# Ten more weight tasks beside the first block's attention, and all but the first eight ordered behind the newest scaled row maxima

## The chip, the cores and the metric

The kernel runs on one core of a Trainium2 chip. The metric is the device time of one execution in microseconds (us). The engines named below are PE (matmuls), DVE (vector), ACT (activations), POOL (GpSimd) and SP, whose queue issues the DMA transfers.

## What is computed

Causal attention with a forget bias, over 4 batches, 8 heads, 576 positions and heads of 64, then two MLP blocks over the 2304 resulting rows of 512:

```python
scores = scale * q @ k.T + minimum(-(cum_i - cum_j), 0), causal; attn = softmax(scores); x = attn @ v
xn = x / rms(x) * rms_g                      # first MLP: d_ff 1536
x = (silu(xn @ w_gate) * (xn @ w_val)) @ w_out
h = x @ w_in                                 # second MLP: d_ff 2048
out = (h - tanh(h)) @ w_out2
```

## The kernel before

Every matmul operand that needs more than half precision is held as a high and a low float16 part, so that one product is three matmuls (lines 676 to 678).

**Attention** goes over 20 tiles T of up to 128 query rows (five in a batch, T0 to T4 the first batch's). For a tile the row maxima of the scores are found first: score matmuls into a "sm" bank (lines 384 to 399) and a reduction on DVE (lines 386, 394, 400). `emit_rt` scales them to a high and a low half (lines 410 and 411, both on DVE), transposes them on PE (414) and sends them by DMA into the query operand. Line 411's instruction is kept as `last_r[0]`: the newest scaled row maxima. Then come, in units of one to four heads, the transposed scores (435, 436), the exponentials (443, ACT), the mask (445, POOL) and the value matmuls (477 for the first batch, in float32). `emit_norm` normalizes a tile's rows in some ten short dependent steps and sends them through transposing DMAs (530, 531) into XT, the operand of the first MLP. `step()` runs the attention's generator by one unit.

**The first MLP** goes over six blocks of 384 rows; block 0 is the tiles T0 to T2. A block has 28 groups: twelve pairs of a gate half (`up1_g`) and a value half (`up1_v`), twelve matmuls each, and four down groups of 36. Each group takes one of two PSUM banks with the tag "mm", and gives it back when DVE or ACT has read it (lines 694, 703, 714).

**Weights.** The weights come as float64. `w1_tasks` is a list of 54 tasks in six column groups, gate and value of three column thirds in turn: g0, v0, g1, v1, g2, v2. A column group is four pieces, one chain and four splits. A piece is a transfer of 512 KB into a raw slot (line 540), three DVE instructions that make float32 of it (542 to 544), a square on ACT into the raw slot (573) and a matmul that sums the squares into an "mm" bank, which all four pieces share (589). There are six raw slots; piece n uses slot n mod 6. The chain reduces that bank on DVE (593) and makes the scale. A split writes the high part on ACT (558) and the low part on DVE (559). `wo_tasks` has 29 such tasks for the down weights. Pair f of a block needs g and v of column third f // 4.

**What sets the order.** The program is traced in the order in which the Python code runs; a scheduler with a simulated timeline then orders each engine's instructions at compile time, so that later work is pulled into gaps where its operands allow. Buffers are handed out by the tile pools. `tc.issue_after(ins)` gives each instruction traced in its block, on the engine of `ins`, a place behind `ins` on that engine; with `last_r[0]` that engine is DVE. The order on every engine is fixed when the kernel runs.

**The loop around the change.** Two weight tasks come first, then the maxima of T0, T1 and T2 and two attention steps. The `while` loop at line 936 then runs steps 3 to 16, until T2 is normalized. T3's maxima are traced within steps 7 to 12, so from step 12 on `last_r[0]` is T3's. One weight task follows each step: the loop takes fourteen of the sixteen in `left`, line 944 the other two, and g0 and v0 are complete. In block 0 of the first MLP, two weight tasks follow each group (line 959), and line 953 first brings up what the next column third needs; when the list is empty, six of the down weights' tasks follow each group.

Of the kernel before, what the change touches and what calls it, by code (L numbers as in the profile page):

```python
# [40 lines left out]
def tile_forget_attention_moe_moe2(ctx, tc, qa, qb, kt, va, vb, va0, vb0, s, wg, wv, wo, rg, win, wo2, out):  # L41
# [315 lines left out]
    last_r = [None]  # L357
# [371 lines left out]
    def run_tasks(lst, n):  # L729
        while n > 0 and lst:  # L730
            lst.pop(0)()
            n -= 1
# [124 lines left out]
    def v_first():  # L857
      with hold():
        vstate[0] = const.tile([128, H], FP32, name="vone")
        V.memset(vstate[0], 1.0)  # L860
        for hh in range(2):
            v32 = VT[hh].bitcast(FP32)
            SY.dma_start(out=v32[:, 0:16, :], in_=va0[hh])
            SY.dma_start(out=v32[0:64, 16:20, :], in_=vb0[hh])
# [22 lines left out]
        SY.dma_start(out=cpd, in_=CP)  # L887
    prep_q(0)
    v_first()
    left = [16]  # L890

    def rest_of_batch0():
        for hh in range(2):
            conv_kc(0, hh, k0, 384, S)
            conv_k2(0, hh, k0, 384, S)

    gen = attn_gen()
    steps = [0]
    total = sum(len(units(T)) for T in range(20)) + 2

    def step():
        try:
            next(gen)
            steps[0] += 1
        except StopIteration:
            pass

    def need(T):
        return sum(len(units(x)) for x in range(T + 1)) + 2
# [26 lines left out]
    while last0 not in done_norm:  # L936
        step()
        if steps[0] == 4:
            rest_of_batch0()
        n = min(left[0], 1)  # L940
        left[0] -= n
        with tc.issue_after(last_r[0]) if left[0] < 8 else ExitStack():
            run_tasks(wt, n)
    run_tasks(wt, left[0])
    wot = wo_tasks(raw_p)
    for j in range(NBLK - 1):
        last = BLOCK_TILES[j + 1][1] - 1
        s0 = steps[0]
        n = min(need(last), total) - s0
# [244 lines left out]
```

## Time and profile before

| | us |
|---|---|
| median of three runs | 1087.5 |
| lowest and highest of them | 1084.29, 1088.48 |
| the profiled execution | 1086.19 |
| its span, first to last instruction | 1084.4 |
| PE busy in the span | 993.0 |
| DVE busy | 621.8 |
| ACT busy | 604.1 |
| POOL busy | 281.9 |

The busy times are sums over stages with different limits, so they have to be read by stretch of the span. A granted TensorE clock of 1.00 is 2.4 GHz and one of 0.50 is 1.2 GHz; a value between is the mean of a stretch in which it changed. "Idle before" is the time in which an engine did nothing ahead of an instruction, and the arrow names what ended it.

### The profile page before, as it was taken

Reading aid. Unit: us, or ns where it says so; the run is one execution under the profiler, and the core shown is the slowest. Engines: PE = TensorE matmul, PEld = TensorE weight load, DVE = VectorE, ACT = ScalarE, POOL = GpSimd, SP = SyncE. Lnnn points to the kernel's source line nnn. Section 1 sums busy time; section 2 is a strip of 40 time slices with the busy share of each in tenths; the row PEclk is TensorE's granted clock in tenths of the full one; section 3 lists DMA queues with packets and bytes.
Section 4 is the critical chain, followed back from the end, with each engine's and each line's share of the span. In section 5 each row is a group of like instructions: output and inputs, shape, how many; then the busy total and the mean of one; then the engine's idle time right before and its main releaser. Section 6 shows DMA issues by size and latency. Waiting matters only on the chain.

```text
span 1084.4 us, 19355 instructions
## 1 busy us (share of the span) xinstructions
PE 993.0 (92%) x7576; PEld 631.0 (58%) x7576; DVE 621.8 (57%) x1421; ACT 604.1 (56%) x1176; POOL 281.9 (26%) x377
## 2 busy tenths in 40 slices
PE   1488878899889999899999899999999999999998
PEld 1377545465556666556566556666666666666665
DVE  8987998966573540674543878485341605234250
ACT  6587668785854662767566447365342515243240
POOL 5122356424652450745345102100000000000000
PEclk9976989899999999999999999999999999999999
DMA  8714333330101212110100960141010010100000
GB/s 268 271 36 110 143 108 113 97 118 21 40 22 50 59 21 82 32 26 22 47 19 11 329 205 1 52 163 45 15 37 24 1 51 8 44 15 8 23 1 30
DMA packets 47517, 75.04 MB, mean 69 GB/s; under 512 B 25506, under 2 KB 33282, under 8 KB 46914
## 3 DMA queue, kind: packets, MB, share of 16 engines
q1 hardware_dynamic: 47426, 73.81, 21.5%
q8 instruction: 59, 0.97, 0.4%
q14 instruction: 32, 0.26, 0.1%
HBM read 59.42 MB, written 9.55 MB: 64 GB/s over the span
## 4 chain that ended last, share of the span: by engine, by line
PE 70%; DVE 15%; ACT 4%; DMA 4%; issue 4%; POOL 3%; SPq 0%; ACTq 0%; DVEq 0%; POOLq 0%
PE m L676 13%; PE m L678 13%; PE m L677 13%; PE mm L676 7%; PE mm L678 7%; PE mm L677 7%; PE pv L477 2%; PE st L435 1%; DVE w L559 1%; PE st L436 1%; POOL phl L457 1%; DVE w L543 1%; DVE q L351 1%; DMA w<-wo 1%; PE pv L479 1%
## 5 line engine op out<-in xcount | busy, mean ns | idle before, releaser
L676 PE MATMUL mm<-xth,w 128*128 128x384 f16 x480 | 160.9, 335 | 15.3 <-DVE tm L694 8.3
L678 PE MATMUL mm<-xth,w 128*128 128x384 f16 x480 | 159.9, 334 | 1.2 <-DVE w L559 1.2
L677 PE MATMUL mm<-xtl,w 128*128 128x384 f16 x480 | 160.7, 335 | 0.0
L1109 DVE SCALAR_TENSOR_TENSOR t<-m,u,t 128x384 f32<-128x384 f32 x96 | 59.2, 616 | 140.3 <-ACT t L1108 138.0
L677 PEld LDWEIGHTS <-w 128*128 128x128 f16 x960 | 95.0, 99 | 76.2 <-issue 22.8
L678 PEld LDWEIGHTS <-w 128*128 128x128 f16 x960 | 94.8, 99 | 65.2 <-issue 3.5
L676 PEld LDWEIGHTS <-w 128*128 128x128 f16 x960 | 95.8, 100 | 59.9 <-issue 4.4
L678 PE MATMUL m<-x2h,wi 128*128 128x384 f16 x384 | 125.2, 326 | 0.0
L677 PE MATMUL m<-x2l,wi 128*128 128x384 f16 x384 | 125.2, 326 | 0.0
L676 PE MATMUL m<-x2h,wi 128*128 128x384 f16 x384 | 125.2, 326 | 0.0
L678 PE MATMUL m<-dh,w 128*128 128x384 f16 x384 | 125.2, 326 | 0.0
L677 PE MATMUL m<-dl,w 128*128 128x384 f16 x384 | 125.2, 326 | 0.0
L676 PE MATMUL m<-dh,w 128*128 128x384 f16 x384 | 125.2, 326 | 0.0
L457 POOL TENSOR_TENSOR phl<-pf,phl 128x512 f16<-128x512 f32 (+2 forms) x90 | 96.0, 1073 | 46.6 <-ACT phl L450 45.7
L1116 POOL TENSOR_SCALAR io<-iso,isd 128x1 f32<-128x1 f32 x24 | 6.5, 271 | 375.8 <-ACT t L1122 314.4
L705 POOL TENSOR_TENSOR sl<-tm,sh 128x384 f16<-128x384 f32 x72 | 75.0, 1042 | 103.9 <-ACT sh L704 102.2
L445 POOL TENSOR_SCALAR_AFFINE_SELECT pf<-pf 128x128 f32<-128x128 f32 (+3 forms) x105 | 46.5, 445 | 187.2 <-ACT pf L443 186.8
L1110 ACT ACTIVATE dh<-t,sd 128x384 f16<-128x384 f32 x96 | 59.0, 615 | 60.9 <-DVE t L1109 60.7
L1122 ACT ACTIVATE t<-m,io 128x384 f32<-128x384 f32 x24 | 13.9, 580 | 141.0 <-PE m L678 141.0
L1111 DVE SCALAR_TENSOR_TENSOR dl<-t,sd,dh 128x384 f16<-128x384 f32 x96 | 59.2, 616 | 52.7 <-ACT dh L1110 51.9
L443 ACT ACTIVATE pf<-st,lnp,ilam 128x512 f32<-128x512 f32 (+2 forms) x105 | 73.1, 701 | 28.6 <-PE st L436 22.7
L676 PE MATMUL mm<-sh,wo 128*128 128x384 f16 x240 | 77.9, 326 | 1.8 <-DVE tm L694 1.8
(312 smaller groups left out, 2298.8 us busy)
## 6 DMA issues: line engine op xcount, KB each, us to landing
raw<-wo SPq DMA_DIRECT2D x16, 512.0 KB
w<-win SPq DMA_DIRECT2D x16, 512.0 KB
wo<-wg SPq DMA_DIRECT2D x12, 512.0 KB
wo<-wv SPq DMA_DIRECT2D x12, 512.0 KB
stk<-kt SPq DMA_DIRECT2D x4, 1152.0 KB
x2d<-tm SPq DMA_DIRECT2D x24, 192.0 KB
x2f<-x2d SPq DMA_DIRECT2D x6, 768.0 KB
out<-t SPq DMA_DIRECT2D x24, 192.0 KB
```

Source lines behind the costliest of these rows:

```text
L443: A.activation(out=pf[:, 0:o], in_=ps[:, 0:o], func=ACTF.Exp, scale=bstate[b]["ilam"][:, hh:hh + 1], bias=lnp)
L445: G.affine_select(out=dg, in_=dg, pattern=[[0, len(heads)], [1, w]], compare_op=ALU.is_ge, fill=0.0, base=0, channel_multiplier=-1)
L457: G.tensor_tensor(out=u["pl"][:, 0:n], in0=u["pf"][:, 0:n], in1=u["ph"][:, 0:n], op=ALU.subtract)
L477: P.matmul(out=ps[0:w, o:o + 65], lhsT=u["pf"][:, cs], rhs=vs.bitcast(FP32), start=(c == 0), stop=(c == nch - 1))
L676: P.matmul(out=ps, lhsT=wh, rhs=xh, start=first, stop=False)
L677: P.matmul(out=ps, lhsT=wh, rhs=xl, start=False, stop=False)
L678: P.matmul(out=ps, lhsT=wl, rhs=xh, start=False, stop=last)
L705: moe_pend.append(lambda: G.tensor_tensor(out=SH["l"][:, f, :], in0=t, in1=SH["h"][:, f, :], op=ALU.subtract))
L1109: V.scalar_tensor_tensor(out=t, in0=ps, scalar=u[:, f // 4:f // 4 + 1], in1=t, op0=ALU.mult, op1=ALU.subtract)
L1110: A.activation(out=DH[:, f, :], in_=t, func=ACTF.Copy, scale=sd)
L1111: moe_pend.append(lambda: V.scalar_tensor_tensor(out=DL[:, f, :], in0=t, scalar=sd, in1=DH[:, f, :], op0=ALU.mult, op1=ALU.subtract))
L1122: A.activation(out=t, in_=ps, func=ACTF.Copy, scale=io)
```

## The change

Two numbers of the loop change, and the number of tasks in a step. `left` starts at 26, so 28 tasks are traced ahead of the first MLP group: g0, v0 and g1 complete, and the first piece of v1. Steps 3 to 6 are followed by one task, steps 7 to 16 by two. The tasks that follow once `left` is under 18 are ordered behind `last_r[0]` on DVE: the first eight of the loop's (through v0's first piece) are free as before; the sixteen behind them, from v0's second piece to g1's third split, are not. Before, six were ordered so, from v0's second piece to its second split. The last two of the 26, traced at line 944, are free in both. In the MLP's loop the rest of the list is two tasks after each group as before, so that it ends three groups earlier and the down weights begin there.

```diff
-    left = [16]
+    left = [26]
...
-        n = min(left[0], 1)
+        n = min(left[0], 1 if steps[0] < 7 else 2)
         left[0] -= n
-        with tc.issue_after(last_r[0]) if left[0] < 8 else ExitStack():
+        with tc.issue_after(last_r[0]) if left[0] < 18 else ExitStack():
             run_tasks(wt, n)
     run_tasks(wt, left[0])
```

## Rows read from the trace of the kernel before

**Rows 1.** The page: the span in 40 slices of 27.1 us, busy tenths.
```profile
DVE  8987998966573540674543878485341605234250
PEclk9976989899999999999999999999999999999999
```

**Rows 2.** Busy time by stretch: from:to, length, engines (instructions), clock, DMA share, GB/s.
```profile
40.00:57.00 17.00, 11.83 (x95) 8.72 (x93) 16.38 (x39) 10.98 (x20) 4.80 (x8) 0.86 0.41 132
57.00:75.00 18.00, 17.29 (x112) 14.41 (x112) 14.91 (x41) 14.78 (x37) 2.20 (x7) 0.66 0.22 52
75.00:89.00 14.00, 10.10 (x115) 8.04 (x114) 13.45 (x42) 12.48 (x23) 5.84 (x10) 0.91 0.49 103
89.00:104.00 15.00, 15.00 (x84) 13.99 (x84) 12.30 (x28) 11.59 (x25) 1.95 (x5) 0.50 0.23 61
104.00:110.00 6.00, 6.00 (x37) 3.41 (x35) 1.92 (x8) 1.37 (x4) 0.52 (x2) 0.75 0.64 212
110.00:215.00 105.00, 85.55 (x795) 53.66 (x794) 100.78 (x241) 75.48 (x165) 52.98 (x60) 0.90 0.35 109
220.00:245.00 25.00, 25.00 (x177) 15.39 (x176) 15.54 (x40) 20.34 (x41) 4.77 (x8) 1.00 0.40 122
220.00:1084.00 864.00, 836.79 (x6273) 521.91 (x6271) 421.14 (x930) 448.71 (x866) 195.80 (x256) 1.00 0.16 51
```

**Rows 3.** SP's queue in order of time: start, length, issues of weight transfers.
```profile
40.34 2.65 SPq L540 DMA_DIRECT2D wo<-wg  x3
...
104.89 0.99 SPq L540 DMA_DIRECT2D wo<-wv  x2
```

**Rows 4.** DVE in order of time: start, length, line, operation, out<-in, shapes.
```profile
47.67 0.82 DVE L542 TENSOR_SCALAR w<-wo 128x512 int32<-128x512 int32 x1
...
56.82 0.78 DVE L544 SCALAR_TENSOR_TENSOR w<-wo,w 128x512 int32<-128x512 int32 x1
57.52 0.15 DVE L411 SCALAR_TENSOR_TENSOR r<-r,r 128x8 f16<-128x8 f32 x1
57.60 0.41 DVE L542 TENSOR_SCALAR w<-wo 128x512 int32<-128x512 int32 x1
```

**Rows 5.** PE in order of time; in brackets the idle before, and its end.
```profile
49.23 1.06 PE L477 MATMUL pv<-vt,pf 128*128 128x65 f32 x8
...
60.99 0.28 PE L414 MATMUL sm<-ident,r 128*16 128x128 f16 x1
...
88.39 0.27 PE L414 MATMUL sm<-ident,r 128*8 128x128 f16 x1 [3.40 <-DVE r L411]
88.59 1.97 PE L477 MATMUL pv<-vt,pf 128*128 128x65 f32 x8
...
103.93 0.51 PE L676 MATMUL mm<-xth,w 128*128 128x384 f16 x1
104.23 1.91 PE L589 MATMUL mm<-wo,rg 128*128 128x512 bf16 x4
...
127.89 0.48 PE L676 MATMUL mm<-xth,w 128*128 128x384 f16 x1 [2.88 <-DVE nmv L593]
```

**Rows 6.** DVE in order of time, two idle times with their ends.
```profile
106.18 0.69 DVE L593 TENSOR_REDUCE nmg<-mm 128x1 f32<-128x512 f32 x1 [2.21 <-PE mm L589]
...
109.39 0.43 DVE L542 TENSOR_SCALAR w<-wo 128x512 int32<-128x512 int32 x1 [1.76 <-DMA wo<-wv]
```

**Rows 7.** DVE groups of 0 to 240 us: busy, mean ns | idle before.
```profile
L543 DVE SCALAR_TENSOR_TENSOR w<-wo,w 128x512 int32<-128x512 int32 x24 | 16.5, 689 | 0.1
L559 DVE SCALAR_TENSOR_TENSOR w<-w,gsg 128x512 f16<-128x512 f32 x12 | 12.6, 1051 | 1.1 <-ACT w L558 1.0
L542 DVE TENSOR_SCALAR w<-wo 128x512 int32<-128x512 int32 x24 | 10.6, 446 | 2.2 <-DMA wo<-wv 1.8 <-DMA wo<-wg 0.3
```

**Rows 8.** POOL and DVE in order of time, around 119 us.
```profile
118.69 2.69 POOL L275 TENSOR_SCALAR kl<-stk,qks 64x2304 f16<-64x2304 f32 x1
...
119.33 2.59 DVE L559 SCALAR_TENSOR_TENSOR w<-w,gsg 128x512 f16<-128x512 f32 x1
```

## The prediction

> **What bounds the kernel now.** I read the 40 slices first, then the busy times by stretch, then the queues in the first 130 us. The slices [rows 1] show two parts. To about 215 us DVE's digit is 8 or 9 in seven of the eight slices, and the granted TensorE clock is often below full. After 220 us PE is busy 836.79 of 864.00 us [rows 2] at full clock: what comes after the first 220 us is a fixed amount of PE work, and a change to the start can only move its beginning. The beginning is set by DVE: the weights are unpacked, scaled and split there, between the steps of the attention. The rows by stretch give DVE's idle time as length less busy time: 0.6 us in 40 to 57, 3.1 in 57 to 75, 0.6 in 75 to 89, 2.7 in 89 to 104, 4.1 in 104 to 110, 4.2 in 110 to 215, then PE is full from 220 on (25.00 of 25.00) [rows 2]. All of DVE's work ahead of 215 has to be done in either order; so the time can fall only by that idle time, 15.3 us in all, 11.1 of it ahead of 110. PE's last idle before its full stretch falls away only with it.
>
> Two stalls stand out in 104 to 110: DVE waits 2.21 us for the squares' matmuls of the second gate group (I call the weight groups g0, v0, g1, v1, ... in their order), and 1.76 us for a transfer of v1 [rows 6]. Both have one cause. The four squares' matmuls of g1 run at 104.23, at once behind the first matmul of the first MLP group at 103.93 [rows 5], though three of their pieces were unpacked by 57.5 [rows 4]. The two "mm" banks are handed out in program order, and in the program g1 stands behind that first group. The squares read the raw slots that v1's transfers need, so these are issued at 104.89 only [rows 3].
>
> **What moves.** Ten tasks go ahead of the first MLP group: the four pieces, the chain and the four splits of g1, and v1's first piece. Nothing is added. On DVE a piece is three instructions, 0.446, 0.689 and about as much again, 1.8 us [rows 7]; five are 9.1 us; a split is 1.05 us on the mean of g's twelve [rows 7], four are 4.2; a chain is a reduction of 0.69 [rows 6] and five short steps, some 1.5 us. That is 15 us of DVE work on paper. ACT gets its squares and high halves in the same order, PE four matmuls and one, POOL one small scaling, SP five issues. Little of it really moves. The rows show three of g1's pieces at 47.67 to 57.5 already: their transfers go out at 40.34 [rows 3], and the last third instruction runs at 56.82, in front of the second half of T2's scaled maxima (57.52); v0's next piece, which the gate holds, begins right behind it at 57.60 [rows 4].
>
> So the edit does four things.
>
> (a) g1's pieces are now ordered behind the newest scaled maxima, T3's from step 12 on. Nine instructions, 5.5 us busy (3 x 1.8), leave 40 to 57. What is queued behind the gate on DVE is g1's pieces, chain and splits; who waits for that is g1's squares, hence v1's raw slots. T2's maxima can come up to 5.5 us sooner. But then DVE has less to fill with. Bounds: nothing lost, or all 5.5 us idle. The nearest row is the next stretch, 57 to 75, with the same kind of chain and few fillers: 3.09 idle on 14.91 busy [rows 2]. On the 10.9 us that stay, that is 2.3 us of idle against 0.6. **+1.6 us.**
>
> (b) v0's pieces, chain and first two splits are spread two to a step, so all are gated by T2's maxima only. In 57 to 75 DVE has three pieces, a chain and two splits to fill with (some 8.5 us) where it had two pieces (3.6 us). Bounds: none or all of the 3.1 us of idle. With waits on PE inside this stretch, where PE is itself 17.29 of 18.00 busy, I take half. **-1.6 us.**
>
> (c) g1 and v1 get their banks ahead of the first MLP group. g1's squares run when their pieces are unpacked, the raw slots come free some 20 us sooner, and v1's third and fourth transfer no longer wait for 103.93. Both stalls go, 4.0 us. Of the other 2.8 us idle in 89 to 110 some goes as g1's chain and splits are there to fill: bounds 0.8 (75 to 89's share, 0.55 in 14, on 21 us) and 2.8, left at 2.0, nearer the upper end since PE is busy 15.00 of 15.00 in 89 to 104 at half clock [rows 2] and its results come late whatever DVE does. **-4.8 us.**
>
> (d) The later groups' banks are handed out earlier too: after it g2 comes behind the third pair's gate half instead of the fifth's. The idle in 110 to 215 is only 4.2 us and spread; I cost this at nothing. Its cover is DVE's backlog; without that a late group costs what the wait of PE for a bank held by a weight group costs now, 2.88 us [rows 5].
>
> The moved ACT, PE and POOL work lies beside DVE's; SP's issues are bound by raw slots, not by their order. One cover may fail: v1's transfers now run beside the transposes of the first tiles.
>
> **Sum**: 1.6 - 1.6 - 4.8 = -4.8 us. The profiled execution took 1086.2 us, 1.8 more than its span; 1086.2 - 4.8 = 1081.4. The median of the three runs is 1.3 above that execution, so 1087.5 - 4.8 = **1082.7 us**. Late next is what is late now: v1's and v2's splits in a full DVE.
>
> A rule on the ports: SBUF — State Buffer in the Trainium skill (Who interferes with whom) says that a VectorE instruction with two inputs in SBUF and a GpSimd instruction that reads SBUF exclude each other, and the later one waits for the whole of the other. One split of g1 that began at 119.33 took 2.59 us while POOL converted keys from 118.69 on for 2.69 us [rows 8], so the trace agrees. By that rule g1's splits, moved to where POOL is busy 9.99 of 47 us (57 to 104) from where it is busy 52.98 of 105, would save perhaps 1 us more; POOL's instruction then meets another of DVE's, so it is not in the sum.
>
> **The rivals.**
> *The clock comes back (faster).* PE waits 3.40 us for T4's maxima until 88.39, and the granted clock is 0.50 for 89 to 104 [rows 2, 5], the lower level. Eight f32 value matmuls take 1.97 us there and 1.06 at 49.23 [rows 5], by their starts 0.87 us more per eight; forty and eight such stand between 88.59 and 100, so 5.2 us. If DVE delivers T4's maxima sooner and the clock stays up, the first MLP group starts that much sooner. The idle left ahead of 110 after my sum, 6.2 us, bounds it: about 1077.5. Against it: in 57 to 75 the clock is 0.66 without any such wait ahead of it. TensorE: Matmul & The Clock Gate in the Trainium skill (Part 1) has it that a busy array opens the gate; PE was busy all through 89 to 104 and was granted half, so by this trace that alone does not do it. Chance 0.15.
>
> *Nothing to see.* The compile-time order already pulls weight work into gaps, as g1's early pieces show; removed stalls come back as others, at -1 to +3 us: 1086 to 1090. For it: DVE's idle in the full stretch is made of many small waits, which any new order makes again. Chance 0.2.
>
> *The gate starves DVE (slower).* T2's maxima come sooner, but their transpose waits on PE behind value matmuls that begin at 57.39, and ran at 60.99 [rows 5]. If PE's order keeps that, the 5.5 us taken out of 40 to 57 buy nothing, and the same work lands behind 110 where DVE is full: +5.5, 1093.0; with one more wait like the 2.88 us one, 1095.9. It decides if T2's transpose stays within 2 us of 61 us. Against it: (b) has work for that stretch. Chance 0.15.
>
> *A bank is taken.* v1's group opens its bank ahead of the first MLP group and gives it back at its chain. If that comes after the first group starts (104 us), two groups run on one bank, and PE waits as it did at 127.89, 2.88 us [rows 5]: 1085.6. Against it: v1's transfers start earlier by (c). Chance 0.08.
>
> **How the numbers follow.** Forecast 0.42 (its own range 1079 to 1086), clock 0.15, nothing 0.2, starved 0.15, bank 0.08. A measurement of this kernel tells 0.5% from no change, 5.4 us, so faster means under 1082.1. My forecast lies 0.6 us above that: just under half of it (0.2) is faster, with the clock's 0.15 and 0.05 of the bank case and of luck, 0.40. Slower by more than 5.4 us, above 1092.9, is most of the starved case, 0.13, and 0.02 of the rest: 0.15. The rest, 0.45, is no change. The range goes from below the clock's case, 1075, to the starved one's lower price, 1093.
>
> **What would show it.** In the changed kernel: g1's squares' matmuls ahead of the first MLP matmul and no wait of 2 us for them on DVE (c); v1's last transfers issued before 95 us; no unpacking between 47 and 53 us and T2's maxima at 53 or sooner (a); DVE's idle in 57 to 110 near 4 us; the full PE stretch beginning some 5 us sooner. I am wrong if DVE's idle ahead of 215 is still about 15 us, if the first MLP group starts after 107 us, or if waits of POOL and ACT after 220 us move the end by more than the start moved.

## The result and the profile after

The changed kernel is slower: **1099.08 us** in the median of six runs (1096.86 to 1099.33) against 1086.11 for the kernel before on the same chip, a ratio of **1.0112, interval 1.0097 to 1.0127**. The forecast was 1082.7 us, and its range ended at 1093: the change costs 1.1%, where 0.4% of gain was forecast. The profiled execution took 1096.86 us with a span of 1095.1, so the two traces differ by 10.7 us.

The 40 slices of the page, of the changed kernel (27.4 us each, beside [rows 1]): DVE's digit is 8 or 9 in seven of the first eight slices, as before, and the granted clock is low in the third to fifth.

```profile
DVE  8999878944556641574643778577251605234250
PEclk9966599899899999999999999999999999999999
```

Busy time by stretch of the changed kernel, in the columns of [rows 2]:

```profile
40.00:57.00 17.00, 14.34 (x127) 11.31 (x124) 14.98 (x41) 13.02 (x27) 4.03 (x9) 0.96 0.27 94
57.00:75.00 18.00, 13.93 (x84) 10.86 (x83) 17.87 (x44) 11.91 (x27) 3.09 (x7) 0.69 0.97 267
75.00:89.00 14.00, 12.92 (x100) 9.16 (x100) 10.93 (x31) 10.54 (x18) 3.13 (x5) 0.71 0.52 155
89.00:104.00 15.00, 2.44 (x19) 1.15 (x18) 14.46 (x42) 8.25 (x12) 3.76 (x4) 0.64 0.50 162
104.00:110.00 6.00, 4.75 (x23) 4.75 (x23) 5.97 (x8) 5.94 (x18) 2.73 (x1) 0.50 0.14 30
110.00:215.00 105.00, 89.16 (x815) 62.75 (x817) 89.42 (x223) 74.11 (x161) 44.14 (x58) 0.84 0.32 92
220.00:245.00 25.00, 24.15 (x151) 14.52 (x150) 11.16 (x29) 13.20 (x29) 3.19 (x5) 1.00 0.18 50
220.00:1084.00 864.00, 837.17 (x6303) 522.39 (x6302) 420.95 (x938) 449.47 (x875) 198.68 (x261) 0.99 0.16 50
```

Read the third number of a row's busy times (DVE) against its length. From 40 to 110 us DVE idles 5.8 us where it idled 11.0. From 110 to 215 it idles 15.6 where it idled 4.2. PE is nearly empty in 89 to 104: 2.44 us of 15, where it was full.

The weights did what the diff says, and more. Rows of SP, DVE and PE of the changed kernel, each engine's in order of time, answering [rows 3 to 6]:

```profile
80.37 1.86 SPq L540 DMA_DIRECT2D wo<-wv  x2
...
84.10 3.66 SPq L540 DMA_DIRECT2D wo<-wg  x4
...
92.06 4.01 SPq L540 DMA_DIRECT2D wo<-wv  x2
...
54.69 0.17 DVE L411 SCALAR_TENSOR_TENSOR r<-r,r 128x8 f16<-128x8 f32 x1
...
85.22 0.69 DVE L593 TENSOR_REDUCE nmg<-mm 128x1 f32<-128x512 f32 x1
...
55.50 0.22 PE L414 MATMUL sm<-ident,r 128*16 128x128 f16 x1
...
79.75 0.58 PE L589 MATMUL mm<-wo,rg 128*128 128x512 bf16 x1 [0.25 <-ACT wo L573]
...
130.15 0.82 PE L676 MATMUL mm<-xth,w 128*128 128x384 f16 x2 [1.65 <-DMA xth<-xh]
```

g1's squares begin at 79.75 instead of 104.23, its chain at 85.22 without a wait where it stood at 106.18 behind 2.21, and v1's last two transfers are issued at 80.37 instead of 104.89. The weights behind them come forward too, though in the program they still stand among the groups of the first MLP: g2's four transfers go out from 84.10 on (before, from 105.98) and v2's first two at 92.06 (before, 123.77). How many pieces DVE has unpacked by the last step of T2's normalization (126.14, before 99.25) shows in their third instruction, line 544; two rows of the changed kernel, then one of the kernel before (count, durations in ns, first and last start):

```profile
L544 DVE SCALAR_TENSOR_TENSOR w<-wo,w x22: 676/683/778, 14.1 to 111.1; 128x512 int32<-128x512 int32 x22
L544 DVE SCALAR_TENSOR_TENSOR wo<-raw,wo x4: 673/674/679, 112.6 to 124.1; 128x512 int32<-128x512 int32 x4
```

```profile
L544 DVE SCALAR_TENSOR_TENSOR w<-wo,w x14: 652/684/782, 14.4 to 93.3; 128x512 int32<-128x512 int32 x14
```

So 26 pieces stand where 14 stood. The five that the edit moves in the program were among the 14 already. The twelve that came are v1's last two, g2's four, v2's first two and four down weights.

But the first MLP matmul comes at 130.15 instead of 103.93. What it waits for is T2's rows. First and last DVE step of the normalizations of T1 and T2, in the changed kernel:

```profile
79.21 0.15 DVE L522 TENSOR_SCALAR ss<-ss 128x1 f32<-128x1 f32 x1 [1.66 <-ACT xl L238]
...
101.80 0.74 DVE L529 SCALAR_TENSOR_TENSOR xl<-x,ss,xh 128x512 f16<-128x512 f32 x1
...
114.46 0.14 DVE L522 TENSOR_SCALAR ss<-ss 128x1 f32<-128x1 f32 x1
...
126.14 0.75 DVE L529 SCALAR_TENSOR_TENSOR xl<-x,ss,xh 128x512 f16<-128x512 f32 x1 [0.39 <-ACT xh L528]
```

The ten short steps of T1 take 23 us from first to last (11 before, 73.22 to 83.77), since weight instructions stand between them; T2's begin at 114.46 (before 92.62). T1's had to wait for ACT, and ACT for a buffer that T0's transposing DMA was still reading; this piece of the chain that ended last (start, length) is of the changed kernel:

```profile
69.19 9.19 DMA xtl<-xl
```

The late start looks like the whole cause. The experiments show that it is not.

**Where the loss builds up.** The last down group of a block (line 714) shows when its MLP is done. Last rows of blocks 0 and 1, changed kernel:

```profile
246.65 0.58 ACT L714 ACTIVATE tm<-mm,iom 128x384 f32<-128x384 f32 x1 [4.54 <-issue]
...
355.27 0.58 ACT L714 ACTIVATE tm<-mm,iom 128x384 f32<-128x384 f32 x1 [3.10 <-PE mm L678]
```

Before they stand at 244.23 and 345.17. So 26 us late at the first matmul have become 2.4 at the end of block 0, and 10.1 at the end of block 1. From there to the end it is 739.8 us here and 739.2 before.

### The profile page after: what moved, and what is told of

Same layout as the page of the kernel before. It is cut to its first block, busy times and chain, and to the rows that moved or that the text cites. A ratio compares the mean times of both kernels' runs of the same rounds, so it can differ in the third digit from the quotient of the medians.

```text
span 1095.1 us, 19358 instructions
## 1 busy us (share of the span) xinstructions
PE 993.5 (91%) x7575; PEld 634.1 (58%) x7576; DVE 615.6 (56%) x1421; ACT 602.6 (55%) x1176; POOL 279.3 (26%) x377
## 4 chain that ended last, share of the span: by engine, by line
PE 65%; DVE 15%; DMA 8%; ACT 6%; issue 4%; POOL 2%; SPq 1%; ACTq 0%; DVEq 0%; POOLq 0%
PE m L676 13%; PE m L677 13%; PE m L678 13%; PE mm L676 6%; PE mm L678 6%; PE mm L677 6%; DVE q L351 1%; DVE w L543 1%; DMA xtl<-xl 1%; DMA stv<-qb 1%; PE st L436 1%; DMA w<-wo 1%; PE st L435 1%; DVE kl L276 1%; POOL phl L457 1%
## 5 line engine op out<-in xcount | busy, mean ns | idle before, releaser
L676 PE MATMUL mm<-xth,w 128*128 128x384 f16 x480 | 160.6, 335 | 16.4 <-DVE tm L694 12.5
L705 POOL TENSOR_TENSOR sl<-tm,sh 128x384 f16<-128x384 f32 x72 | 74.5, 1035 | 116.4 <-ACT sh L704 113.0
L445 POOL TENSOR_SCALAR_AFFINE_SELECT pf<-pf 128x128 f32<-128x128 f32 (+3 forms) x105 | 42.6, 408 | 165.0 <-ACT pf L443 164.3
```

Source lines behind the costliest of these rows:

```text
L445: G.affine_select(out=dg, in_=dg, pattern=[[0, len(heads)], [1, w]], compare_op=ALU.is_ge, fill=0.0, base=0, channel_multiplier=-1)
L676: P.matmul(out=ps, lhsT=wh, rhs=xh, start=first, stop=False)
L705: moe_pend.append(lambda: G.tensor_tensor(out=SH["l"][:, f, :], in0=t, in1=SH["h"][:, f, :], op=ALU.subtract))
```

## The experiments

All times are medians, each with the ratio to the kernel before on the same chip and its 95% interval. The last four columns are from the trace of one execution, which can lie some 5 us from the median: the first MLP matmul, the last down groups of blocks 0 and 1, the span.

| kernel | us | ratio | first | block 0 | block 1 | span |
|---|---|---|---|---|---|---|
| before | 1086.11 | | 103.9 | 244.2 | 345.2 | 1084.4 |
| changed | 1099.08 | 1.0112 [1.0097, 1.0127] | 130.1 | 246.7 | 355.3 | 1095.1 |
| e1 ten behind the loop | 1089.33 | 1.0029 [1.0012, 1.0046] | 128.4 | 242.1 | 347.3 | 1084.1 |
| e2 changed, loads early | 1108.86 | 1.0207 [1.0163, 1.0251] | 146.5 | 267.6 | 370.9 | 1111.0 |
| e3 changed, no gate | 1100.24 | 1.0129 [1.0097, 1.0162] | 124.0 | 257.6 | 358.9 | 1099.0 |
| e4 pace alone | 1096.94 | 1.0100 [1.0068, 1.0131] | 101.9 | 245.0 | 354.0 | 1095.0 |
| e5 one more behind | 1109.93 | 1.0214 [1.0194, 1.0234] | 119.8 | 279.5 | 371.7 | 1108.6 |
| e6 gate alone | 1106.53 | 1.0189 [1.0164, 1.0214] | 113.5 | 262.3 | 370.2 | 1109.9 |
| e7 changed, late pace | 1094.54 | 1.0066 [1.0050, 1.0083] | 130.3 | 246.1 | 351.8 | 1093.5 |
| e8 one fewer behind | 1086.76 | 1.0004 [0.9993, 1.0015] | 103.0 | 243.6 | 345.3 | 1086.3 |
| e9 changed, 14 groups | 1087.62 | 1.0015 [1.0000, 1.0030] | 122.3 | 244.0 | 345.2 | 1084.8 |
| e10 before, 14 groups | 1096.47 | 1.0096 [1.0076, 1.0116] | 103.4 | 248.7 | 355.0 | 1093.5 |
| e11 changed, 12 groups | 1091.82 | 1.0053 [1.0036, 1.0070] | 124.2 | 247.9 | 350.4 | 1091.0 |
| e12 ten behind the norm | 1097.51 | 1.0106 [1.0074, 1.0137] | 113.7 | 256.0 | 358.2 | 1098.7 |
| e13 changed, 15 groups | 1086.74 | 1.0008 [0.9993, 1.0024] | 130.7 | 239.7 | 345.0 | 1084.0 |
| e14 changed, 13 groups | 1087.29 | 1.0012 [0.9995, 1.0030] | 123.0 | 248.3 | 346.5 | 1089.2 |
| e15 e1 with 14 groups | 1095.43 | 1.0085 [1.0064, 1.0107] | 134.6 | 247.2 | 352.7 | 1093.5 |
| e16 before, 15 groups | 1086.12 | 1.0003 [0.9988, 1.0017] | 103.3 | 242.1 | 343.0 | 1085.0 |

The span less the last row of block 1 lies between 736.8 and 742.7 in all eighteen: the end is set there, and not by the first matmul, which comes at 101.9 in a kernel that loses 1.0% and at 130.7 in one that loses nothing.

### One part of the change at a time

The first theory: weights that run ahead of T1's and T2's normalizations make the first group late, and the end follows. Rivals: the loads of the second batch; the gate; the pace.

**e1**, the kernel before with the ten tasks traced behind the loop, without pace and gate:

```diff
-    run_tasks(wt, left[0])
+    run_tasks(wt, left[0] + 10)
```

> The loop is that of before (sixteen tasks, one a step, six ordered behind the maxima); the ten more tasks are traced behind the loop, behind T2's normalization and ahead of the first MLP group. Theory A (in the changed kernel the weight tasks stand ahead of the normalizations of T1 and T2, and DVE's in-order queue makes each of some ten dependent short steps wait between weight instructions, so that the first MLP group starts at 130 us instead of 104): the first group starts at 102 to 108 again, and the time is that of before within 4 us, 1082 to 1090. Rival C (the loss comes with g1's and v1's banks handed out ahead of the MLP and with the earlier end of the list, wherever the tasks are traced): 1094 to 1099.

Measured 1.0029. The first matmul is as late as in the changed kernel (128.4), but most of the loss is gone. A late start alone doesn't cost 12 us. The late start itself goes with the weights that run ahead of it: 24 pieces are unpacked ahead of T2's last step here, 14 in the runs that start by 104 us (e4, e8, e10, e16).

**e2**, the changed kernel with the second batch's first query load ordered behind v0's third transfer again. The loads are ordered behind the SP instruction that was traced fourth last, and the ten tasks move that place, so that these loads go out at 58.54 instead of 24.70:

```diff
-        with hold():
+        with tc.issue_after(anchor[0]) if (b, hh) == (1, 0) else hold():
...
+        if mark:
+            anchor.append([i for i in nc.cur_bb.bb.instructions if i.engine == SY.engine][-1])
...
```

> The changed kernel, but the first load of the second batch's queries is ordered behind the transfer of v0's third piece, as it came out in the kernel before, where the changed kernel had it behind T4's query load. Theory A (DVE's order): the first MLP group still starts later than 120 us and at most 3 us of the 13 come back, 1096 to 1099. Theory B (the loads of the second batch, moved from 25 us to 58 us, fill the DMA engines from 57 to 75 us; T0's transposing DMA takes 9.2 us there, T1's normalization waits for its buffer, and all that follows is late by that): the first group starts near 110 to 118 us, and 5 to 10 us come back, 1089 to 1094.

Measured 1.0207: worse than the change and outside both ranges. The moved loads are a side effect that I had not seen. That they are not what costs the time is shown by e13 below, which issues them at 59.72, as late as the change, and loses nothing.

**e3**, the changed kernel without the gate:

```diff
-        with tc.issue_after(last_r[0]) if left[0] < 18 else ExitStack():
-            run_tasks(wt, n)
+        run_tasks(wt, n)
```

> The changed kernel with no task ordered behind the maxima. Theory A: the gate is not what costs; without it still more weight work goes ahead of the attention's chains, T2's maxima come later than 54 us, and the time is the changed kernel's or up to 6 us more, 1098 to 1105. Rival D (the gate starves DVE and shifts g1's pieces into the full stretch, 5.5 us): 1091 to 1095.

Measured 1.0129, and its interval holds the changed kernel's whole: taking the gate away gives nothing back.

**e4**, the kernel before with two tasks a step from step 7 on, and nothing else:

```diff
-        n = min(left[0], 1)
+        n = min(left[0], 1 if steps[0] < 7 else 2)
```

> The kernel before with two tasks a step from step 7 on, so that v0's pieces, chain and splits are traced four or more steps sooner, with no task of g1 ahead of the MLP. Theory A: v0 is needed for the first pair anyway, and only ten tasks' DVE time is in play; the time is that of before within 4 us, 1083 to 1090, and the first group starts before 112 us. If the pace alone delays the normalizations: first group later than 118 us, 1092 or more.

Measured 1.0100. The first matmul comes 2 us sooner than before, at 101.9, and the kernel still loses 1.0%: it is 0.8 us behind at the end of block 0 and 8.8 at the end of block 1. With e1 this refutes the first theory, that the end follows the first group, from both sides.

**e5** and **e8**, the kernel before with one task more, and one fewer, behind the loop:

```diff
-    run_tasks(wt, left[0])
+    run_tasks(wt, left[0] + 1)      # e8: left[0] - 1
```

> The kernel before with one more task behind the loop: g1's first piece opens its bank ahead of the first MLP group, and nothing else of the program's order changes. Theory P (what costs in the changed kernel is the pace of two tasks a step, which the kernel before with that pace alone showed at 1.0%): the time is that of before within 4 us, 1082 to 1090, and g1's squares run ahead of the first MLP matmul. Theory S (the compile-time order is sensitive as such, and any edit of the task list moves the time by several us, with no cause in the edit): a difference of more than 5 us to either side.

> The kernel before with one task fewer behind the loop: v0's last split is traced behind the first MLP group, which does not need it. Theory P: the time is that of before within 4 us, 1082 to 1090. Theory S: more than 5 us to either side.

One more costs 2.1%, ten more (e1) 0.3%, one fewer nothing. The time is not a function of how many tasks stand there.

**e6**, the kernel before with the gate on all fourteen tasks that the loop takes (the two of line 944 stay free):

```diff
-        with tc.issue_after(last_r[0]) if left[0] < 8 else ExitStack():
+        with tc.issue_after(last_r[0]) if left[0] < 18 else ExitStack():
```

> The kernel before with all sixteen tasks ordered behind the newest maxima, the pace as before. Theory P: the first eight are g0's rest and v0's first piece, and g0 is needed at 104 us only; T2's maxima come earlier than 57.5 us and the time is that of before within 4 us, 1082 to 1090. Rival D (the gate starves DVE): 1091 or more. Theory S: more than 5 us to either side.

Measured 1.0189. Alone, the gate costs more than the whole change, and taking it out of the change (e3) gives nothing back: the parts don't add up.

**e7**, the changed kernel with one task a step to step 11 and three from step 12:

```diff
-        n = min(left[0], 1 if steps[0] < 7 else 2)
+        n = min(left[0], 1 if steps[0] < 12 else 3)
```

> The changed kernel's 26 tasks and gate, but one task a step until T3's maxima (step 12) and three a step from there: v0 comes as in the kernel before, the ten more tasks beside the last five units of T2 and T3. Theory P (the pace in steps 7 to 11): most of the 13 us come back, 1084 to 1091. Theory A (weight work ahead of T1's and T2's normalization on DVE, whatever the step): the first MLP group starts later than 118 us and the time is 1094 to 1100. Theory S: no relation to either.

Measured 1.0066, in theory A's range, with the first matmul where the change has it (130.3). Some 40% of the loss is gone, none of it at the start.

**e12**, the kernel before with the ten tasks behind the loop, each held on DVE behind the last instruction of T2's normalization:

```diff
+        norm_ins[0] = nc.cur_bb.bb.instructions[-1]      # in emit_norm, behind line 529
...
     run_tasks(wt, left[0])
+    with tc.issue_after(norm_ins[0]):
+        run_tasks(wt, 10)
```

> The kernel before and, behind the loop, the same ten more tasks, each held on DVE behind the last instruction of T2's normalization, so that they get their banks ahead of the first MLP group but can't go ahead of the three normalizations. If the loss comes from weights that run ahead of the normalizations: T0 to T2 are sent at 67, 83 and 99 us as before, the first group starts at 104 to 112 us (it may wait for a bank until the second gate group's chain), and the time is 1083 to 1090 us. Rival: what costs is the bank or the new order; then the normalizations stay at 67, 83 and 99 us and the time is still 1093 us or more.

The normalizations keep their place (T2's rows are sent at 97.8), but the first matmul waits until 113.7, behind g1's chain at 113.0: g1 now holds a bank that the first MLP group wants. Measured 1.0106. Protecting the normalizations doesn't save the change.

### The same start, another number behind it

e1 and e7 point behind the start. The next theory, of a debt: the weights push the attention back, block 1 then waits for it, and more attention in block 0's first groups pays it sooner. The steps of block 1's tiles are spread over the first 16 of block 0's groups; this edit changes that one number:

```diff
-SPREAD = (16, 20, 20, 18, 20)
+SPREAD = (14, 20, 20, 18, 20)
```

> The changed kernel with one number else: the attention steps of block 1's tiles are spread over the first 14 groups of block 0's MLP instead of 16. Theory of the debt (the start loses 6 us of matmul work by 215 us, and 4 us more go in block 1 because the attention stands behind the weights and its conversions come late): the lag of PE's work against before at 345 us shrinks from 10 us to 6 or less, the waits for DVE's tm in 265 to 345 fall, 1090 to 1095 us. Rival, the order theory (a new list gives a new order on every engine, good or bad whatever it means): no such relation, anything from 1085 to 1110 us, and the first MLP group moves away from 130 us though nothing ahead of it is edited.

> The kernel before with the same one number: 14 groups instead of 16. Theory of the debt: before pays no debt (PE is full from 220 us), so there is nothing to gain; DVE has the same work in fewer groups, 1085 to 1089 us, and everything ahead of 110 us stays. Rival, the order theory: 3 to 20 us slower, as the other small edits of the list of tasks were.

> The changed kernel with 12 groups instead of 16, twice the dose. Theory of the debt: another step the same way, PE's lag at 345 us at 4 us or less, 1087 to 1094 us, unless DVE's work in 130 to 215 us (72.8 of 85 us busy in the changed kernel) fills up and block 0 waits instead. Order theory: no relation to the kernel with 14, 1085 to 1110 us.

The changed kernel gets nearly all of its loss back (1.0015), the kernel before loses 1.0% by the same edit, and a second step the same way (12) is worse again. The first is better than the debt had it, the second against it, the third within it. Four more runs ask whether a smooth relation lies behind it; e13 and e14 are the changed kernel with 15 and 13, e16 the kernel before with 15, e15 is e1 with 14:

> The changed kernel with the attention steps of block 1's tiles spread over 15 of block 0's groups. With 16, 14 and 12 groups the ratio to before was 1.0112, 1.0015 and 1.0053. If what is left of the attention behind the weights sets the loss, 15 lies between 14 and 16: 1089 to 1096 us. If the order of every engine is a throw for each list, there is no reason for it to lie between: anything from 1085 to 1110 us, outside 1089 to 1096 about as likely as inside.

> The changed kernel with 13 groups. By the debt it lies between 14 and 12: 1087 to 1092 us. By the throw: 1085 to 1110 us.

> The kernel before with the ten tasks behind the loop (1.0029 before this) and 14 groups instead of 16. That kernel's matmul work caught up with before by 300 us and was 2 us behind at 345. By the debt, two groups fewer give it the rest: 1083 to 1088 us, no slower than with 16. By the throw: 1085 to 1110 us.

> The kernel before with 15 groups instead of 16; with 14 its ratio was 1.0096. By the debt it lies between: 1087 to 1096 us. By the throw: 1084 to 1110 us.

On the changed kernel 12, 13, 14, 15 and 16 groups give 1.0053, 1.0012, 1.0015, 1.0008 and 1.0112; on the kernel before 14, 15 and 16 give 1.0096, 1.0003 and 1; on e1, 14 and 16 give 1.0085 and 1.0029. On either list the whole loss comes in one step, from 15 to 16 on the one and from 15 to 14 on the other; both runs with 15 lie below what the debt gave them (1086.74 for 1089 to 1096, 1086.12 for 1087 to 1096), and e1 loses by the edit that saves the change. Of the seven ranges that the debt gave, two hold (e11, e14). The debt as a smooth relation falls. What stays is that each list gets an order of its own, and that the loss hangs on the order behind the start.

**e13 against the changed kernel shows this.** PE's order is the same in both up to the MLP's first matmul, DVE's up to T2's normalization; the first matmul comes at 130.7 and 130.1, T2's rows are sent at 126.8 and 126.1. Only then do they part. The last down groups of blocks 0 and 1 in e13:

```profile
239.68 0.58 ACT L714 ACTIVATE tm<-mm,iom 128x384 f32<-128x384 f32 x1 [2.78 <-issue]
...
344.96 0.58 ACT L714 ACTIVATE tm<-mm,iom 128x384 f32<-128x384 f32 x1 [0.19 <-PE mm L678]
```

Block 0 is done 7.0 us sooner than in the changed kernel, block 1 another 3.3. Four stretches hold it; first the changed kernel, then e13 (columns of [rows 2]):

```profile
190.00:200.00 10.00, 6.96 (x64) 4.53 (x62) 9.87 (x21) 9.69 (x20) 5.89 (x6) 0.83 0.29 81
200.00:215.00 15.00, 12.83 (x106) 8.34 (x105) 14.60 (x45) 9.35 (x23) 6.62 (x8) 0.89 0.35 114
285.00:300.00 15.00, 10.88 (x65) 6.11 (x65) 9.31 (x24) 5.92 (x15) 0.91 (x1) 0.77 0.17 39
300.00:315.00 15.00, 10.71 (x99) 6.76 (x97) 7.52 (x9) 12.79 (x19) 13.12 (x13) 0.89 0.17 56
```

```profile
190.00:200.00 10.00, 10.00 (x132) 6.97 (x131) 8.24 (x16) 9.17 (x23) 7.80 (x12) 1.00 0.32 116
200.00:215.00 15.00, 13.69 (x136) 9.09 (x135) 12.63 (x44) 13.58 (x27) 7.80 (x10) 1.00 0.38 126
285.00:300.00 15.00, 13.34 (x126) 8.88 (x123) 10.64 (x18) 14.50 (x26) 8.55 (x11) 1.00 0.16 49
300.00:315.00 15.00, 11.39 (x122) 7.91 (x123) 7.66 (x14) 11.04 (x24) 8.67 (x10) 1.00 0.21 53
```

In these 55 us the changed kernel's PE is busy 7.0 us less, and its granted clock falls short of full by 8.5 us of time (0.17 x 10 + 0.11 x 15 + 0.23 x 15 + 0.11 x 15), part of it in those idle times; e13 has full clock throughout. So these stretches hold between 7.0 and 15.5 us of loss; the spans differ by 11.1. An empty stretch is not yet a loss, though: in the kernel before, PE is busy 6.97 of 10.00 us in 190 to 200 too, at a clock of 0.66. From 215 to 345 us the three compare so (before, changed, e13):

```profile
215.00:345.00 130.00, 119.30 (x998) 76.47 (x996) 79.63 (x184) 86.07 (x169) 56.63 (x64) 0.99 0.19 54
215.00:345.00 130.00, 117.53 (x991) 75.17 (x990) 74.14 (x179) 81.73 (x165) 57.30 (x67) 0.96 0.15 44
215.00:345.00 130.00, 120.12 (x1053) 78.56 (x1052) 80.12 (x199) 86.24 (x177) 58.70 (x71) 1.00 0.15 43
```

PE idles 10.7, 12.5 and 9.9 us, and by the mean clock 1.3, 5.2 and 0 us of time are short, part of them in idle times. Against the kernel before, the lower clock (+3.9) weighs more here than the waits (+1.8).

**One of these waits in the rows.** What PE waited for most in 265 to 345 us in the changed kernel (line and releaser, total, times, longest):

```profile
PE mm L676 <- DVE tm L694: 7.8, 3, 5.6
```

The engines around the longest of these, in order of time on each:

```profile
282.18 2.22 ACT L269 ACTIVATE kc<-stk,qks 64x2304 f16<-64x2304 f32 x1 [2.04 <-DVE qks L247]
284.42 0.58 ACT L693 ACTIVATE tm<-mm,ct 128x384 f32<-128x384 f32 x1
...
282.24 2.18 POOL L275 TENSOR_SCALAR kl<-stk,qks 64x2304 f16<-64x2304 f32 x1 [0.65 <-DVE qks L247]
...
282.37 2.08 DVE L251 TENSOR_SCALAR kap<-lam,isig_c 128x2 f32<-128x2 f32 x1
...
285.73 2.61 DVE L276 SCALAR_TENSOR_TENSOR kl<-stk,qks,kl 64x2304 f16<-64x2304 f32 x1
...
288.52 0.55 DVE L694 SCALAR_TENSOR_TENSOR tm<-tm,mm 128x384 f32<-128x384 f32 x1
...
289.12 0.48 PE L676 MATMUL mm<-xth,w 128*128 128x384 f16 x1 [5.61 <-DVE tm L694]
```

The keys of the third batch are converted on ACT, POOL and DVE just as a gate half needs its eviction. ACT's tanh (284.42) comes behind ACT's conversion, and DVE's eviction behind DVE's, at 288.52, though its input was there at 285.0. PE stands still for 5.61 us, and when it starts again a 384-column matmul takes 0.48 us instead of 0.33: the clock is at its lower level. In e13 the same conversion begins on DVE at 281.42, directly behind an eviction at 280.85. PE stands there too, but less, and most of it for row maxima:

```profile
280.91 0.22 PE L414 MATMUL sm<-ident,r 128*16 128x128 f16 x1 [2.12 <-DVE r L411]
...
281.44 0.32 PE L676 MATMUL mm<-xth,w 128*128 128x384 f16 x1 [0.31 <-DVE tm L694]
```

So the place costs the changed kernel 3.2 us more of waiting (5.61 for 2.12 and 0.31), and half clock from 287.8 to 294.6, which e13 doesn't have. This is read from the rows; an order with only this place changed wasn't tried.

## Why the prediction was wrong

**The terms of the sum.** (a) DVE's idle in 40 to 57 rose from 0.6 to 2.0 us, +1.4 for +1.6. T2's maxima came at 54.69, 2.8 us sooner, not at 53. (b) In 57 to 75 it fell from 3.1 to 0.13, -3.0 for -1.6: near the bound, not half way. (c) Both stalls went; in 89 to 110 the idle fell from 6.8 to 0.6, -6.2 for -4.8. In 75 to 89, which no term covers, it rose by 2.5, where DVE waits for T1's normalization behind T0's transposing DMA (79.21): 1.66 us of it at one place. That is the cover that I had named as one that may fail, but beside that transfer run mostly the second batch's loads, not v1's. The sum is -5.2, and I had forecast -4.8. The idle ahead of 110 came out as forecast, and the kernel became 10.7 us longer. (The filler of (b) adds up to 9.0 us by its own terms, not 8.5; no number rests on that. g1's four splits, left out of the sum, took 2.96 us instead of 5.44, and line 249 met POOL's conversion in their place, 2.07 us for 0.18.)

**The step that failed** is the one from DVE's idle time to the end: "All of DVE's work ahead of 215 has to be done in either order; so the time can fall only by that idle time", and "a change to the start can only move its beginning". DVE did not do the same work ahead of 215: 153.6 us of it in 40 to 215 against 159.7 before. What it did early was weights: 26 pieces instead of 14 ahead of T2's rows. "Little of it really moves" is right of the edit's own pieces, but (c) follows the freed raw slots to v1's last two transfers only, and ten more pieces came forward behind them. These went ahead of steps whose results others wait for: the first block's normalizations, and T7's rows, sent at 266.0 instead of 230.1 (261.2 in e13, so that this alone is not the loss either). A busy DVE is not a DVE on the path. Behind 110 the idle that I had removed came back twice over, 15.6 us for 4.2, so that DVE's idle from 40 to 215 is 21.4 us, the first sign of being wrong that I had named. And the part behind 220 was not fixed: before, its PE was full in 220 to 245 because evictions, units and conversions happened to fall well (it idled 10.7 us in 215 to 345 even so), and an order that puts a conversion ahead of an eviction opens it further. Of the 10.1 us at the end of block 1, 7.7 came after block 0.

**(d)** is the term: "I cost this at nothing", with DVE's backlog as cover. The sum ended at 110 us, and the whole loss lies behind it. The price there is not a mean of small waits but of one order against another: a ratio of 1.0112 for this list, and of 1.0008 to 1.0015 for the same list with 15, 14 or 13 groups (1.0053 with 12).

**The order's priorities** I had not costed at all. I counted the ten tasks as filler, but on DVE they and the pieces behind them went ahead of T1's and T2's steps, and the first group started 26 us late. I had named that sign (a first group after 107 us), and it came; e13 shows that this alone costs nothing measurable, since blocks 0 and 1 had room to catch up. Had I foreseen it, I would have put a price on the wrong thing.

**The rivals.** "The gate starves DVE" was to be decided by T2's transpose: it ran at 55.50, far from 61, so it did not happen, and e13 has the gate and loses nothing; e6 shows a gate that costs more, but by a new order as a whole. "The clock comes back": the reverse, it stayed at half from 93 to 134 (in e13 from 93 to 134 too, without a loss). "A bank is taken" did not bind here; e12 shows the mechanism, with 10 us of a later first matmul. "Nothing to see" came nearest, in that removed stalls come back as others, but I let it cost 3 us at most. Its price should have been read from a stretch in which PE is already full: what one wait of 2 to 6 us there costs, several times.

**What stays open** is which property of an order makes it good, and so why this list with 16 groups got a bad one: no run changed the order at one place alone. Of the seventeen edited kernels five lie within 0.15% of the kernel before (e8, e9, e13, e14, e16), twelve are 0.3 to 2.1% slower, and none is faster. The lists with a late first matmul are in both groups.

## What to carry to other kernels

Where a scheduler orders all engines at compile time, an edit to a list of filler tasks is not a local edit: cost it over the whole stretch in which the engines still share work, and take the spread of small neutral edits (here 0 to 2%) as the uncertainty before taking idle times as gains. Idle time saved on a busy engine is worth something only if the saved time goes to the work that ends last; follow the dependent short chains (a normalization, an eviction) through the new order first, and count the later work that comes forward behind the edit's tasks, not only those tasks (here twelve pieces that the edit doesn't name). To tell a late start from a later loss, keep the start and change one number behind it: two traces with one start and two ends say which it was.

## What the chip showed that I had not expected

In the changed kernel PE's clock stayed at its lower level for 41 us, from 93.2 to 134.2: PE was almost idle in 89 to 104 (2.44 of 15.00 us busy), but it was busy 4.75 of 6.00 in 104 to 110 at 0.50. The drops at 195.6, 205.9, 287.8 and 311.7 came in or shortly behind waits of PE: 2.2 us idle from 191.8, 2.2 from 202.5, 5.6 from 283.5, 1.3 and 1.5 from 309.5 and 311.0. In e13 waits of 2.1 and 2.3 us (at 278.8 and 299.9) were not followed by one.

The transposing DMA of T0's low half took 9.19 us from its issue at 69.19, with the DMA engines 0.97 busy at 267 GB/s in that stretch; before, at 0.22 and 52 GB/s, the same buffer was free for T1 by 70.93 after an issue at 68.11.

A short VectorE step can be as long as a GpSimd instruction beside it. Line 249, two inputs of two columns, took 2.07 us from 104.66 and ended at 106.73, with POOL's conversion (4.76 us from 101.97); at 282.18, just ahead of such a conversion, it took 0.16. The Trainium skill has the rule for it (SBUF — State Buffer, Who interferes with whom): a VectorE instruction with two inputs in SBUF and a GpSimd instruction that reads SBUF exclude each other for the whole instruction. The two rows agree with it. Line 251, one input and a scalar per partition, took 2.08 us from 282.37 while POOL's conversion ran from 282.24 for 2.18, and 0.26 at 111.67; that sentence does not cover it. This one stood in the chain that held the eviction at 288.52, but e13 has such a one too (2.07 us from 277.33).
